# Padding between SBUF tiles, whole-chunk transposes and a new pitch for the hidden features in an attention and mixture-of-experts kernel

## The chip, the cores and the metric

The kernel runs on one core of one Trainium2 chip. The metric is the device time of one execution in microseconds (us). Before the change it is 820.12 us, the median of three runs (819.98 to 822.11).

In a profile PE is TensorE (PEld its weight loads), DVE is VectorE, ACT is ScalarE, POOL is GpSimd and SP is SyncE, whose queue starts most DMAs. L551 is line 551 of the kernel before. In the changed file the lines from 531 to the transposes are one later: L551 is L552 there, and L970 is L971.

## The reference

Three parts follow each other: a causal attention with a decay, a gated dense layer, and eight experts of which each token uses one.

```python
# attention: B, H, S, D = 4, 8, 576, 64
scores = q @ k.T / sqrt(D) + cum[:, None] - cum[None, :]     # cum = cumsum(log(clip(f)))
attn = softmax(where(causal, -1e9, scores)); attn_out = attn @ v
# dense: x has 2304 tokens of 512 features; w1, w2: 512 x 1024; w3: 1024 x 1024; w_out: 1024 x 512
x = ((x @ w1) * (x @ w2)) @ w3 @ w_out
# experts: w1[e]: 512 x 1024, w2[e]: 1024 x 512
e = argmax(x @ w_gate); gate = softmax(x @ w_gate)[e] * sigmoid(x @ w_output_gate)[e]
out = gate * (relu(x @ w1[e]) @ w2[e])
```

Nearly every product is computed in three matmuls on operands that were split into a high and a low part: high times high, high times low, low times high. The split is made by a copy into TensorE's rounded float format (the high part, names with h) and a subtraction of that copy from the value (the remainder or low part, names with l).

## The kernel before

**Attention** takes 16 pairs of heads in a software pipeline whose order is written out by a table of start times. While it runs, pieces of w3 and w_out are read and split as well. The matmuls at L515 to L517 (`product`) then multiply w3 by w_out, so that the dense layer needs one matrix less; their results have the name wc.

**The dense layer** (`gated`, `project`) takes tokens in tiles of 512, 512, 512, 512 and 256. For each tile and each of 8 pieces of the hidden width, 12 matmuls make x @ w1 (name a) and 12 make x @ w2 (name b): 4 pieces of the contraction times the three products of `three` (L551 to L553). ScalarE and VectorE multiply the two and split the product into gh and gl. Then `project` makes the rows y: for each chunk of 128 tokens, 8 pieces times three matmuls with gh or gl as weights and the combined matrix (raw) streaming through. In the first tile the split of w1 and w2 is still going on: VectorE makes the low parts at L467, one pair per piece of the hidden width. The first tile's own split of x is at L571 (ScalarE, high part) and L572 (GpSimd, low part).

**Routing** finds each token's expert and scatters its row to a list per expert in DRAM (L710). The expert with most tokens is done first, in pieces A (256 tokens) and B (128). Seven slots follow, with 344, 320, 320, 296, 280, 256 and 256 tokens each, then a small piece p, then a loop that is empty with this input.

**One slot**: `fetch` reads its token rows from DRAM, in chunks of 128 rows; `features` turns them on TensorE (transposes with the identity, L970), in two runs of two feature blocks each; `layer1` (name h) has 96 matmuls of as many columns as the slot has tokens; `layer2_turned` (name q, 96 matmuls of that width) or `layer2` (name o, 24 matmuls of 512 columns for each chunk of 128 tokens) makes the output rows, which GpSimd scatters. Slots with 320, 320, 296 and 280 tokens use q; A, B and the slots with 344, 256 and 256 use o. Weights of the next slot are read and split meanwhile (`load`, L544 on GpSimd and L545 on VectorE).

**Order.** In this part TensorE and VectorE run in the order in which the code records them (`manual_schedule`). TensorE takes its matmuls strictly in that order; each of them has a weight load of its own, and the load of the next one is done beside the running matmul.

**Where the tiles lie.** Tiles of a pool lie behind each other in SBUF, from the low end or, with side="right", from the high end. The built programs place the start of each tile as follows. Only the remainder modulo 512 bytes is given, and one column of a float32 tile is 4 bytes:

```
tiles                                                        before   after
raw0, raw1 (combined matrix; b weights of odd slots)            128     384
big: w1, w2, gh, gl of the dense layer; other expert weights     32     384
xh, xl of the dense layer's tokens (high end of SBUF)           384     384
cw: the first pieces of w_out and w3                            384     384
gh, gl of an expert slot (pitch 344 columns = 1376 bytes)  416, 288  128, 0
hh, hl of an expert slot (before always pitch 344)         160, 416 384, 128
attention: CK, MR, OQ, tri, junk, PT, vr, ac, ones ...   all 256 higher
attention: kh, kl, qh, ql, kr, qr                             not moved
```

Within raw, big, xh, xl and cw the operands are 512 or 2048 bytes apart, so each of them has the remainder of its tile. The rows of 344 columns are not a whole number of 512 bytes, so each block there has another remainder.

Of the kernel before, what the change touches and what calls it, by code (L numbers as in the profile page):

```python
# [28 lines left out]
P = 128  # L29
# [490 lines left out]
def moe(nc, tc, ident, xT, rz, xs, xpool, raws, region, wc, w1, w2, gates, e1, e2, out):  # L520
# [3 lines left out]
    with (  # L524
# [3 lines left out]
    ):  # L528
        psum = ExitStack()
        st = {"work": wc.work, "unit": 1}  # L530

        def unit(name, n, dt=F32R):

# [428 lines left out]
        def features(nm, g, w):  # L962

            xh = pmb.tile([P, 4, WIN[1]], F32R, name=f"gh{nm}", tag="gxh")
            xl = pmb.tile([P, 4, WIN[1]], F32R, name=f"gl{nm}", tag="gxl")
            yield xh, xl
            for k in range(4):
                pt = mmt(f"gt{nm}{k}") if nm in "A1B" else psx.tile([P, 512], F32, name=f"gt{nm}{k}", tag="x")
                for c, n in chunks(w):
                    PE.transpose(pt[:, P * c:P * c + n], g[0][:n, c, P * k:P * k + P], ident[:n, :n])  # L970
                A.activation(out=xh[:, k, :w], in_=pt[:, :w], func=ACTF.Copy)  # L971
                V.tensor_tensor(out=xl[:, k, :w], in0=pt[:, :w], in1=xh[:, k, :w].bitcast(F32), op=ALU.subtract)
                yield

        def hidden(nm):
            return (pmb.tile([P, 8, WIN[1]], F32R, name=f"hh{nm}", tag="hh"),
                    pmb.tile([P, 8, WIN[1]], F32R, name=f"hl{nm}", tag="hl"))

        def layer1(nm, ws, x, w, h):
            (wh, wl), (xh, xl), (hh, hl) = ws[0], x, h  # L980
# [124 lines left out]
        with tc.manual_schedule(engines={PE_E, DVE_E}):  # L1105
            wm, gA = weights("m", m), fetch("A", rows_of_expert(m), 256)
            fA = features("A", gA, 256)
            xA, hA = next(fA), hidden("A")
            rest = project(len(TT) - 1, TT[-1] // P)
            load(4)  # L1110
            take(fA, 2)
# [25 lines left out]
            run(l1)  # L1137
            y = layer2("A", wm, gA, hA, 256)
            fB = features("B", gB, P)
            xB, hB = next(fB), hidden("B")  # L1140
            run(y)
            run(fB)
            load(2)
# [6 lines left out]
            load(2)  # L1150
            run(layer2("B", wm, gB, hB, P))
            load(1)
            h = hidden("1")
            l1 = layer1("1", ws, x, WIN[1], h)
            for _ in range(3):
                take(l1, 1)
# [2 lines left out]
            for i in range(1, E):  # L1159
                nm, w = str(i), WIN[i]  # L1160
                if i == E - 1:
                    pe0 = nc.values_load(tab[0:1, E:E + 1], engines=SPE, min_val=0, max_val=E - 1)
                    px0 = nc.values_load(tab[0:1, E + MAXP:E + MAXP + 1], engines=SPE, min_val=0, max_val=E * N - R)
                    nm2, e2_, w2_, rows2 = "p", pe0, R, lambda r, n: xs[bass.ds(px0, n)]
                else:
                    nm2, e2_, w2_, rows2 = str(i + 1), slots[i + 1], WIN[i + 1], rows_of_expert(slots[i + 1])
                g2 = fetch(nm2, rows2, w2_)
                ws2 = (weights if i < E - 1 else plain)(nm2, e2_)
                if i > 1:
                    h = hidden(nm)  # L1170
                    l1 = layer1(nm, ws, x, w, h)
                    take(l1)
                for k in range(4):
                    take(l1, 2 if i > 1 else 1)
                    load(1 if i < E - 1 else 0)
                run(l1)
                fx = features(nm2, g2, w2_) if i < E - 1 else iter(())
                x = next(fx, None)
                take(fx, 2)
                y = (layer2_turned if w % P and w <= TURNED else layer2)(nm, ws, g, h, w)  # L1180
                if i < E - 1:
                    take(y)
                    take(fx, 2)
                    for k in range(4):
                        load(1)
                        take(y)
                        take(pl)
                else:
                    x = turned_piece("p", g2)
                    take(y)  # L1190
                    p = piece("p", ws2, g2, x)
                    for _ in range(2):
                        take(p)
                        take(y)
                run(y)
                ws, g = ws2, g2
# [32 lines left out]
def program(shapes):  # L1229
# [3 lines left out]
    with tile.TileContext(nc) as tc:  # L1233
        with tc.tile_pool(name="keep", bufs=1) as keep, tc.tile_pool(name="raws", bufs=2, reuse_waits="tile") as raws, tc.tile_pool(name="div", bufs=1, space=DRAM) as div:
            rz = div.tile([NP, 2, N], F32, name="rz")

            xs = div.tile([E * N, DM + 2], F32, name="xs")
            ident = keep.tile([P, P], F32, name="ident")
            make_identity(nc, ident)
            xpool = ExitStack()  # L1240
            xt = xpool.enter_context(tc.tile_pool(name="xt", bufs=1, side="right"))
            xT = xt.tile([P, NP, N], F32, name="xT")
            region = ExitStack()
            region.enter_context(tc.manual_schedule())
            wc = Combined(nc, tc, xpool, raws, a["wo"], a["w3t"])
            attention(nc, tc, ident, xT, rz, xs, wc, a["q"], a["k"], a["v"], a["f"])
            moe(nc, tc, ident, xT, rz, xs, xpool, raws, region, wc, a["w1"], a["w2"], a["gates"], a["e1"], a["e2"], out)
            xpool.close()
# [10 lines left out]
```

## Time and profile before

| | before |
|---|---|
| median of three runs | 820.12 us (819.98 to 822.11) |
| profiled execution | 821.04 us, its span 819.43 us |
| PE busy | 790.8 us (97%), 5173 matmuls |
| DVE busy | 458.2 us (56%) |
| POOL busy | 349.2 us (43%) |
| ACT busy | 281.6 us (34%) |
| DMA | 102.12 MB, mean 125 GB/s |

The span is what the profiler saw of the device's work, and 1.61 us of the time lie around it. Busy shares are means over stages that differ a lot, so the stage tables below are of more use than this one. A matmul's own duration in the profile overlaps the next one's, so what a matmul costs is the distance from its start to the next start, or the length of a stretch over the matmuls in it.

### The profile page before, as it was taken

Reading aid. Unit: us, or ns where it says so; the run is one execution under the profiler, and the core shown is the slowest. Engines: PE = TensorE matmul, PEld = TensorE weight load, DVE = VectorE, ACT = ScalarE, POOL = GpSimd, SP = SyncE. Lnnn points to the kernel's source line nnn. Section 1 sums busy time; section 2 is a strip of 40 time slices with the busy share of each in tenths; the row PEclk is TensorE's granted clock in tenths of the full one; section 3 lists DMA queues with packets and bytes.
Section 4 is the critical chain, followed back from the end, with each engine's and each line's share of the span. In section 5 each row is a group of like instructions: output and inputs, shape, how many; then the busy total and the mean of one; then the engine's idle time right before and its main releaser. Section 6 shows DMA issues by size and latency. Waiting matters only on the chain.

```text
span 819.4 us, 13839 instructions
## 1 busy us (share of the span) xinstructions
PE 790.8 (97%) x5173; PEld 645.2 (79%) x5173; DVE 458.2 (56%) x971; ACT 281.6 (34%) x536; POOL 349.2 (43%) x362
## 2 busy tenths in 40 slices
PE   8999999998999999999999999999899999999995
PEld 4666667676888887887788788898697999999983
DVE  6788888985999723241341322346367746445520
ACT  2566666553556312212211221313121222322221
POOL 6678889996640210230221011033454443445511
PEclk9999999999999999999999999999999999999998
DMA  3556767524545110110100010044676546547470
GB/s 104 157 156 188 225 213 248 148 67 146 189 155 180 52 40 27 39 38 1 65 7 13 20 39 0 2 151 144 185 242 208 167 176 198 162 166 230 140 267 29
DMA packets 40339, 102.12 MB, mean 125 GB/s; under 512 B 8610, under 2 KB 9314, under 8 KB 40016
## 3 DMA queue, kind: packets, MB, share of 16 engines
q1 hardware_dynamic: 37088, 91.46, 35.2%
q0 software_dynamic: 3184, 9.77, 3.1%
q8 instruction: 41, 0.67, 0.3%
q14 instruction: 26, 0.21, 0.1%
HBM read 84.47 MB, written 16.51 MB: 123 GB/s over the span
## 4 chain that ended last, share of the span: by engine, by line
PE 71%; DVE 10%; DMA 6%; issue 6%; POOL 5%; ACT 1%; SPq 1%; POOLq 0%; DVEq 0%; ACTq 0%
DVE junk L243 6%; PE a L551 4%; PE b L551 4%; PE b L552 4%; PE a L552 4%; PE y L552 4%; PE y L551 4%; PE y L553 4%; PE b L553 4%; PE a L553 4%; PE h L553 3%; PE h L551 3%; PE h L552 3%; PE q L551 2%; DMA out<-ot,id 2%
## 5 line engine op out<-in xcount | busy, mean ns | idle before, releaser
L581 DVE TENSOR_TENSOR ga<-b,ga 128x512 f32<-128x512 f32 (+1 forms) x40 | 25.5, 637 | 149.6 <-PE b L553 148.7
L710 POOL DMA_INDIRECT xs<-xr,pos x18 | 19.0, 1056 | 182.0 <-DVE pos L706 130.6
L243 DVE CUSTOM_DVE_ANT_0 junk<-x,tri 128x256 f32<-128x256 f32 (+3 forms) x128 | 62.7, 490 | 10.6 <-PE x L217 1.5
L551 PE MATMUL h<-gh,ah 128*128 128x320 f32 (+4 forms) x224 | 67.2, 300 | 0.0
L552 PE MATMUL h<-gl,ah 128*128 128x320 f32 (+4 forms) x224 | 66.9, 299 | 0.0
L553 PE MATMUL h<-gh,al 128*128 128x320 f32 (+4 forms) x224 | 66.9, 299 | 0.0
L551 PE MATMUL b<-xh,w2h 128*128 128x512 f32 (+1 forms) x160 | 60.5, 378 | 0.0
L551 PE MATMUL a<-xh,w1h 128*128 128x512 f32 (+1 forms) x160 | 60.3, 377 | 0.0
L552 PE MATMUL b<-xl,w2h 128*128 128x512 f32 (+1 forms) x160 | 60.0, 375 | 0.0
L552 PE MATMUL a<-xl,w1h 128*128 128x512 f32 (+1 forms) x160 | 60.0, 375 | 0.0
L553 PE MATMUL b<-xh,w2l 128*128 128x512 f32 (+1 forms) x160 | 59.3, 371 | 0.0
L553 PE MATMUL a<-xh,w1l 128*128 128x512 f32 (+1 forms) x160 | 59.3, 370 | 0.0
L544 POOL TENSOR_SCALAR bh<-rb 128x1024 fp32r<-128x1024 f32 x28 | 37.0, 1323 | 49.0 <-DMA rb<-e 43.9
L285 POOL TENSOR_SCALAR_AFFINE_SELECT PT<-PT 128x256 f32<-128x256 f32 (+1 forms) x80 | 45.6, 584 | 28.9 <-ACT PT L279 27.0
L551 PE MATMUL y<-raw,gh 128*128 128x512 f32 x144 | 57.6, 400 | 0.0
L552 PE MATMUL y<-raw,gh 128*128 128x512 f32 x144 | 57.0, 396 | 0.0
L553 PE MATMUL y<-raw,gl 128*128 128x512 f32 x144 | 56.7, 393 | 0.0
L583 ACT ACTIVATE gh<-ga 128x512 fp32r<-128x512 f32 (+1 forms) x40 | 23.6, 589 | 90.8 <-DVE ga L581 90.8
L986 DVE SCALAR_TENSOR_TENSOR hl<-h,hh 128x320 fp32r<-128x320 f32 (+4 forms) x56 | 25.4, 463 | 48.0 <-ACT hh L985 46.3
L306 PE MATMUL v<-PT,vr 128*64 128x448 f32 (+4 forms) x384 | 49.8, 396 | 1.1 <-ACT zs L329 1.1
L545 DVE TENSOR_TENSOR bl<-rb,bh 128x1024 fp32r<-128x1024 f32 x28 | 37.9, 1376 | 15.0 <-POOL bh L544 15.0
L297 POOL TENSOR_TENSOR ac<-ac,PT 128x640 f32<-128x640 f32 (+1 forms) x32 | 45.6, 1424 | 1.6
(611 smaller groups left out, 2177.6 us busy)
## 6 DMA issues: line engine op xcount, KB each, us to landing
ra<-e SPq DMA_DIRECT2D x28, 512.0 KB
rb<-e SPq DMA_DIRECT2D x28, 512.0 KB
w<-w3t SPq DMA_DIRECT2D x16, 512.0 KB
xs<-zero SPq DMA_DIRECT2D x8, 771.0 KB
vr<-v SPq DMA_DIRECT2D x16, 320.0 KB
kr<-k SPq DMA_DIRECT2D x16, 288.0 KB
qr<-q SPq DMA_DIRECT2D x16, 288.0 KB
wo<-wo SPq DMA_DIRECT2D x8, 512.0 KB
```

The lines of the kernel that those rows point to most:

```text
L243: V.tensor_tensor_reduce(out=junk[:, :w], in0=s["x", i][:, 512 * h:512 * h + w] if i < 4 else s["x", i][:, 224:224 + S], in1=tri[:, 640 - ...
L285: G.affine_select(out=t, in_=t, pattern=[[0, 2], [1, w]], compare_op=ALU.is_ge, fill=0.0, base=0, channel_multiplier=-1,)
L297: G.tensor_tensor(out=acc[:, :, q0 - P:], in0=first if j == 1 else acc[:, :, q0 - P:], in1=src, op=ALU.add)
L306: PE.matmul(s["v"][HALF[h], 384 + q0:384 + q1], s["vr"][:, j, HALF[h]], place(s, j, h, q0, q1), start=(j == 0), stop=(j == 4 or q1 == P),)
L544: G.tensor_scalar(out=hi, in0=src, scalar1=1.0, scalar2=1.0, op0=ALU.mult, op1=ALU.mult)
L545: lo_eng.tensor_tensor(out=lo, in0=src, in1=hi.bitcast(F32), op=ALU.subtract)
L551: PE.matmul(ps, ah, bh, start=start and i == 0, stop=False)
L552: PE.matmul(ps, ah, bl, start=False, stop=False)
L553: PE.matmul(ps, al, bh, start=False, stop=stop and i == last)
L581: V.tensor_tensor(out=ga[:, :w], in0=pb[:, :w], in1=ga[:, :w], op=ALU.mult)
L583: A.activation(out=gh[:, f, :w], in_=ga[:, :w], func=ACTF.Copy)
L986: V.scalar_tensor_tensor(out=hl[:, f, :w], in0=ps[:, :w], scalar=0.0, in1=hh[:, f, :w].bitcast(F32), op0=ALU.max, op1=ALU.subtract)
```

## The change

It is described as three changes: tiles at one address modulo 512 bytes, whole-chunk transposes of gathered rows, and the first tile's remainders on VectorE.

- Three tiles that nothing uses are added as padding (24 columns in pool mo2, 72 in mob, 64 in keep), and with them the tiles lie as in the table above.
- The hidden features of a slot of at most 256 tokens have a pitch of 256 columns instead of 344; the calls of `hidden` hand over the number of tokens.
- The transposes of the last chunk of a slot's rows take all 128 rows instead of the slot's last 88, 64, 40 or 24. The rows were read by `fetch` before as well; the copies behind the transposes read the same columns as before.
- For the third part there is no edit in the diff. The split at L571 and L572 is the same in both files.

```diff
@@ moe
         st = {"work": wc.work, "unit": 1}
+        p2.tile([P, 24], F32, name="shift2", bufs=1)
@@ features
-                for c, n in chunks(w):
-                    PE.transpose(pt[:, P * c:P * c + n], g[0][:n, c, P * k:P * k + P], ident[:n, :n])
+                for c, _ in chunks(w):
+                    PE.transpose(pt[:, P * c:P * c + P], g[0][:, c, P * k:P * k + P], ident)
@@ hidden
-        def hidden(nm):
-            return (pmb.tile([P, 8, WIN[1]], F32R, name=f"hh{nm}", tag="hh"),
-                    pmb.tile([P, 8, WIN[1]], F32R, name=f"hl{nm}", tag="hl"))
+        def hidden(nm, w):
+
+            pitch = WIN[-1] if w <= WIN[-1] else WIN[1]
+            made = [pmb.tile([P, 8 * WIN[1]], F32R, name=f"{x}{nm}", tag=x) for x in ("hh", "hl")]
+            if "shift" not in st:
+                st["shift"] = pmb.tile([P, 72], F32, name="shift3")
+            return tuple(t[:, :8 * pitch].rearrange("p (f c) -> p f c", c=pitch) for t in made)
...
@@ program
             ident = keep.tile([P, P], F32, name="ident")
+            keep.tile([P, 64], F32, name="shift")
```

The order of instructions moves in one place of its kind on one engine. On PE, between the last matmuls of layer 1 of the slot with 344 tokens (h) and the first of its layer 2 (o), the transposes (gt) of the next slot's gathered rows (xg, 320 tokens) stood like this before:

```order
L553 MATMUL h_6274<-gh_5997,al_5864 128x344
L970 MATMUL gt_6291<-ident,xg_6182 128x128 x2
L970 MATMUL gt_6291<-ident,xg_6182 128x64
L970 MATMUL gt_6297<-ident,xg_6182 128x128 x2
L970 MATMUL gt_6297<-ident,xg_6182 128x64
L551 MATMUL o_6303<-bh_5865,hh_6079 128x512
```

and stand like this now:

```order
L554 MATMUL h_6277<-gh_6000,al_5867 128x344
L971 MATMUL gt_6294<-ident,xg_6185 128x128 x3
L971 MATMUL gt_6300<-ident,xg_6185 128x128 x3
L552 MATMUL o_6306<-bh_5868,hh_6082 128x512
L553 MATMUL o_6306<-bl_5869,hh_6082 128x512
```

The number of transposes is the same; the third of each three is 128 columns wide instead of 64. There are ten such runs, two for each of the slots with 344, 320, 320, 296 and 280 tokens.

On POOL, in the part where the last pieces of w3 and w_out are split (L467) and the first tile's x is split, the low parts of that tile (xl) stood like this before:

```order
L467 TENSOR_TENSOR raw_76<-wo7u,raw_76 128x512
L572 TENSOR_TENSOR xl_2994<-xT,xh_2993 128x512 x2
L467 TENSOR_TENSOR raw_77<-w07u,raw_77 128x512
L572 TENSOR_TENSOR xl_2994<-xT,xh_2993 128x512
L467 TENSOR_TENSOR raw_77<-w17u,raw_77 128x512
```

and stand like this now:

```order
L467 TENSOR_TENSOR raw_77<-wo7u,raw_77 128x512
L573 TENSOR_TENSOR xl_2996<-xT,xh_2995 128x512 x2
L467 TENSOR_TENSOR raw_78<-w07u,raw_78 128x512
L573 TENSOR_TENSOR xl_2996<-xT,xh_2995 128x512
L467 TENSOR_TENSOR raw_78<-w17u,raw_78 128x512
```

Nothing moved there: the remainders stay on GpSimd. DVE, ACT, POOL and SP have the same instructions in the same order in both programs, apart from line and buffer numbers.

## Rows read from the trace of the kernel before

**Rows 1.** Stages of the span: us, then busy (count) by engine, PEclk, DMA share, GB/s.
```profile
0.00:193.34 193.34, 177.17 (x1813) 123.84 (x1814) 161.05 (x397) 109.05 (x173) 159.02 (x172) 0.99 0.54 168
193.34:237.14 43.80, 43.80 (x196) 36.16 (x193) 37.27 (x42) 22.25 (x39) 27.76 (x18) 1.00 0.48 156
237.14:519.14 282.00, 282.00 (x1268) 224.89 (x1266) 111.54 (x253) 74.74 (x145) 44.28 (x48) 1.00 0.13 44
519.14:601.58 82.44, 78.62 (x514) 68.09 (x512) 41.83 (x123) 22.04 (x59) 26.51 (x39) 1.00 0.42 132
601.58:810.82 209.24, 209.24 (x1393) 192.26 (x1391) 106.46 (x158) 53.03 (x121) 90.65 (x85) 1.00 0.57 189
```

**Rows 2.** Groups of 512-column matmuls by line and shape: busy us, mean ns.
```profile
L551 PE MATMUL y<-raw,gh 128*128 128x512 f32 x144 | 57.6, 400 | 0.0
...
L551 PE MATMUL b<-xh,w2h 128*128 128x512 f32 x128 | 51.2, 400 | 0.0
L551 PE MATMUL a<-xh,w1h 128*128 128x512 f32 x128 | 51.0, 399 | 0.0
```

**Rows 3.** Stretches of 512-column matmuls: wc, wc, wc, a and b, y.
```profile
204.35:215.24 10.89, 10.89 (x49) 9.01 (x48) 10.23 (x12) 4.89 (x9) 6.71 (x4) 1.00 0.56 182
218.00:228.88 10.88, 10.88 (x49) 9.01 (x48) 10.85 (x11) 6.05 (x11) 8.95 (x6) 1.00 0.50 165
228.88:231.69 2.81, 2.81 (x13) 2.26 (x12) 2.81 (x2) 1.19 (x2) 2.35 (x2) 1.00 0.25 102
237.14:281.94 44.80, 44.80 (x193) 36.04 (x192) 40.71 (x71) 24.97 (x43) 1.32 (x2) 1.00 0.44 141
281.94:293.14 11.20, 11.20 (x49) 8.96 (x48) 8.80 (x25) 1.23 (x2) 8.16 (x10) 1.00 0.04 4
```

**Rows 4.** Stretches of narrower matmuls: a and b of 256, q of two 320 slots.
```profile
533.91:545.43 11.52, 11.52 (x98) 11.52 (x97) 3.40 (x8) 3.21 (x8) 1.95 (x2) 1.00 0.54 182
651.01:654.64 3.63, 3.63 (x26) 3.62 (x25) 2.01 (x4) 0.44 (x1) 2.38 (x2) 1.00 0.66 176
...
682.84:686.46 3.62, 3.62 (x26) 3.61 (x26) 1.99 (x4) 0.42 (x1) 2.25 (x2) 1.00 0.66 171
```

**Rows 5.** Timeline of PE at four runs of transposes: start, us, line, operation, count.
```profile
593.57 0.76 PE L970 MATMUL gt<-ident,xg 128*128 128x128 f32 x6
594.17 0.49 PE L1006 MATMUL htB<-ident,hrB 128*128 128x128 f32 x3
...
616.73 1.15 PE L970 MATMUL gt<-ident,xg 128*128 128x128 f32 x6
617.80 0.50 PE L551 MATMUL o<-bh,hh 128*128 128x512 f32 x1
...
716.92 1.08 PE L970 MATMUL gt<-ident,xg 128*128 128x128 f32 x6
717.94 0.41 PE L551 MATMUL q<-hh,bh 128*128 128x296 f32 x1
...
767.57 0.60 PE L970 MATMUL gt<-ident,xg 128*128 128x128 f32 x4
767.92 0.48 PE L551 MATMUL o<-bh,hh 128*128 128x512 f32 x1
```

**Rows 6.** Timeline of DVE, then PE: last weights of the first dense tile.
```profile
273.52 1.74 DVE L467 TENSOR_TENSOR w1l<-wa7u,w1h 128x512 fp32r<-128x512 f32 x1
...
276.81 0.39 PE L553 MATMUL a<-xh,w1l 128*128 128x512 f32 x1
```

**Rows 7.** Timeline of PE where it waits between pieces A and B.
```profile
577.56 0.51 PE L551 MATMUL oA<-bhm,hhA 128*128 128x512 f32 x1 [1.05 <-POOL bhm L544]
...
587.13 0.66 PE L970 MATMUL gtB<-ident,xgB 128*128 128x128 f32 x4 [1.28 <-DMA xgB<-xs]
```

**Rows 8.** The group of the page that the attention waits for most.
```profile
L243 DVE CUSTOM_DVE_ANT_0 junk<-x,tri 128x256 f32<-128x256 f32 (+3 forms) x128 | 62.7, 490 | 10.6 <-PE x L217 1.5
```

More of the change, by code (lines that the diff above doesn't have):

```diff
@@ L1107, in moe @@
             fA = features("A", gA, 256)
-            xA, hA = next(fA), hidden("A")
+            xA, hA = next(fA), hidden("A", 256)
             rest = project(len(TT) - 1, TT[-1] // P)
@@ L1139, in moe @@
             fB = features("B", gB, P)
-            xB, hB = next(fB), hidden("B")
+            xB, hB = next(fB), hidden("B", P)
             run(y)
@@ L1152, in moe @@
             load(1)
-            h = hidden("1")
+            h = hidden("1", WIN[1])
             l1 = layer1("1", ws, x, WIN[1], h)
@@ L1169, in moe @@
                 if i > 1:
-                    h = hidden(nm)
+                    h = hidden(nm, w)
                     l1 = layer1(nm, ws, x, w, h)
```

## The prediction

> **What bounds the kernel now.** I read the busy time by stage first [rows 1]. [...] From 519.14 to 601.58 PE is idle for 82.44 - 78.62 = 3.8 us, at waits inside the pieces A and B. Before 193.34 us the attention is a chain through all engines; PE is busy for 177 of 193 us there and DVE for 161, and no single engine's speed sets it. Behind PE's last matmul stand 8.6 us of copy, scatter and closing. [...]
>
> **What a matmul costs, and what address has to do with it.** Next I compared stretches with the same work in each matmul (512 columns, a 128 x 128 weight load beside it) and different addresses [rows 3]. A stretch counts one matmul that began before it, so its number is the count less one.
> - 204.35 to 215.24 us: 48 matmuls in 10.89 us, 226.9 ns each. The streaming operand lies at 384 modulo 512, the weights at 128: 256 apart.
> - 218.00 to 228.88 us: 48 in 10.88 us, 226.7 ns. Both at 32.
> - 228.88 to 231.69 us: 12 in 2.81 us, 234.2 ns. Same line, same loop, weights at 128 and streaming at 32.
> - 237.14 to 281.94 us (a and b of the first tile): 192 in 44.80 us, 233.3 ns. Weights at 32, streaming at 384.
> - 281.94 to 293.14 us (y): 48 in 11.20 us, 233.3 ns. Weights at 32, streaming at 128.
> [...] The third line decides for me that it is the address: it stands in the middle of the same product and differs in nothing else that I see. After the change all of raw, big, xh, xl and cw lie at 384, so a, b and y should run at 226.7.
>
> [...]
>
> **The change part by part**, each on PE's path.
> 1. a and b of the four tiles of 512: 6 groups of 128 matmuls, 768 [rows 2], by 233.3 - 226.7 = 6.6 ns: -5.1 us.
> 2. y: 3 groups of 144, 432 [rows 2], by 6.6 ns: -2.9 us.
> 3. a and b of the last tile: 192 of 256 columns, 120.0 ns each (96 in 11.52 us) [rows 4]. No row shows this width at equal addresses. Bounds: nothing, and the same 6.6 ns (-1.3 us). I take half, as the columns are half: -0.6 us.
> 4. o: with pitch 256 the weights hh and hl lie at 384 or 128 and the streaming weights of the slot at 384, so equal modulo 256. The two slots of 256 tokens and B have 48 + 48 + 24 = 120 such matmuls: -0.8 us. A has 48 more, but PE waits in them for bhm, and behind them for the gather xgB [rows 7]; both hang on scatters, not on PE's speed. So A gains nothing. The slot with 344 tokens keeps its pitch, where each block has another remainder: 0.
> 5. q (384 matmuls): the hidden features keep pitch 344, so their blocks go through all remainders, whatever the weights' is. The rows have the test: the slot at 651.01 us has weights at 32 and needs 3.63 us for its first quarter, that at 682.84 us has them at 128 and needs 3.62 [rows 4]. I take 0.
> 6. h (768 with A): streaming gh and gl have pitch 344, and their remainders against the weights' only change places. Taken 0; no row has another arrangement, so the bounds are 6.6 ns scaled to some 300 of 512 columns, 3.9 ns each, 3.0 us to either side.
> 7. The wc stretch at 228.88 us: -0.1 us.
> 8. Transposes. A run of six with 64 or fewer columns in the last chunk takes 1.07 us from its start to the next matmul's (616.73 to 617.80), in the slot of 280 tokens 1.02 (716.92 to 717.94) [rows 5]; the eight such runs take 1.07, 1.10, 1.08, 1.08, 1.05, 1.04, 1.02 and 1.02, together 8.46 us. The run with 88 columns in the last chunk takes 0.60 (593.57 to 594.17), and four whole ones 0.35 (767.57 to 767.92). So the narrow ones do not save columns; they cost some 0.2 us each. Six whole ones are bounded by 1.5 x 0.35 = 0.53 and by 0.60 with two wider transposes, 0.66. I take 0.59: 8 x 0.59 = 4.7, so -3.7 us (bounds -4.2 and -3.2). The two runs of the 344 slot change by less than 0.1 us.
> [...]
>
> Sum: -(5.1 + 2.9 + 0.6 + 0.8 + 0.1 + 3.7) = -13.2 us.
>
> **What could be late next.** VectorE makes the weights of the first dense tile while PE uses them. The last low part of w1 ends at 273.52 + 1.74 = 275.26 us and is first needed at 276.81 [rows 6]. PE reaches that place 7 x 24 x 6.6 ns = 1.1 us earlier, with 0.1 from part 7: 1.55 - 1.2 leaves 0.3 us. That just holds. If VectorE's part comes 1 us late, 1 us is lost once. The gathers, scatters and weight loads around A and B start when PE or engines behind it are done, so they move along; only what PE gains between two of their steps is lost, which part 4 has left out.
> Third part of the description: nothing in the program does it, so it is 0 for certain.
> Attention: the two operands of each matmul there move together, or one moves by 256, so no pair changes modulo 256; DVE's, ACT's and POOL's work is the same. 0.
>
> The sum is made on the profiled execution: 821.04 - 13.2 = 807.8 us. That execution is 0.92 us above the median of the runs, to which the result will be compared: 820.12 - 13.2 = 806.9 us, which I forecast.
>
> **The rivals.**
> - *Address does not matter.* wc goes to another PSUM bank after each three matmuls, a and b put 12 and y 24 into one, and that might make the difference. Then only the transposes count: 820.1 - 3.7 = 816.4 us. Against it stands the stretch at 228.88 us, which changes banks too and is slow. Chance 0.08.
> - *The gain is partly swallowed by waits.* VectorE limits the first tile (1.3 us of part 1), and the last tile's gain ahead of A (part 3, and 48 of the y: 0.9 us) goes into longer waits there: 806.9 + 2.2 = 809.1 us. For it: the margin of 0.3 us. Against it: the weights and the scatters follow PE. Chance 0.15.
> - *h gains as well*, since remainders that change places need not cost the same: 806.9 - 3.0 = 803.9 us. Nothing in the rows speaks for it. Chance 0.06.
> - *Slower than before.* In the attention 256 bytes move the tiles of VectorE's scan for maxima (junk, tri) against the tiles at the high end of SBUF. If engines meet in SBUF by address as TensorE's two reads do, these instructions, 128 of 490 ns (62.7 us, on the chain) [rows 8], would stretch. They must cost 13.2 us more, that is 21%, before the kernel is slower; at 25% it would be 822.6 us. For it: the chain waits for VectorE there. Against it: their operands move by the same 256 bytes, and nothing else about them changes. Chance 0.03.
>
> **How the numbers follow.** The forecast has 0.68, the rivals 0.32. The likeliest one's own range is 804 to 810 us (parts 3, 6 and 8 with their bounds). With the swallowed gain, 803.5 to 811.5 us; outside are the first and the last rival and some of the tails, 0.2. About 0.3% (2.5 us) is what this measurement can tell from no change. The forecast and three rivals are faster than that, the first rival by only 3.7 us, so that a part of it may read as no change: faster 0.93, same 0.04, slower 0.03.
>
> **What would show it.** In the changed kernel's profile a and b of the first tile should take 43.5 us instead of 44.80 for 192 matmuls, and y 10.88 instead of 11.20 for 48; a run of six transposes 0.6 us everywhere; an o of the last slots 226.7 ns a matmul. PE should have no idle time between 193 and 519 us, and waits of about the same length at A and B. q and h should stay within 1% per matmul. It is wrong if a and b stay at 233 ns (first rival), if PE shows idle time in the first tile (second), if h changes by more than 2 ns a matmul, or if the attention does not end at 193 us within 1 us.

## The result and the profile after

The changed kernel takes 809.49 us (median of four runs, 808.69 to 811.58), beside 820.05 us of the kernel before (four runs, 818.91 to 822.11). The ratio is 0.9872, with a 95% interval of 0.9845 to 0.9899. A second comparison (the last experiment below) gave 808.79 against 820.10 us, 0.9854 with 0.9824 to 0.9884. So 10.6 and 11.3 us went, where 13.2 were forecast; 809.49 lies inside the stated range (803.5 to 811.5), 2.6 us above the forecast of 806.9.

The stages of the changed kernel's profiled execution (808.69 us, span 807.0), cut at the same instructions as [rows 1] and with the same columns:

```profile
0.00:192.15 192.15, 176.75 (x1812) 123.26 (x1814) 160.46 (x397) 108.84 (x173) 158.05 (x172) 1.00 0.54 169
192.15:235.80 43.65, 43.65 (x196) 36.14 (x193) 35.34 (x40) 20.31 (x36) 26.55 (x18) 1.00 0.47 147
235.80:512.07 276.27, 275.82 (x1267) 224.66 (x1266) 112.33 (x255) 76.28 (x147) 45.04 (x48) 1.00 0.13 46
512.07:593.70 81.63, 77.89 (x513) 68.11 (x512) 41.96 (x123) 22.06 (x59) 26.39 (x39) 1.00 0.42 132
593.70:798.42 204.72, 204.72 (x1393) 191.81 (x1391) 105.97 (x159) 52.05 (x121) 87.31 (x85) 1.00 0.59 193
```

Stage by stage the difference is -1.2 us (attention), -0.15 (product), -5.7 (dense tiles of 512), -0.8 (last tile, A and B) and -4.5 (the seven slots): 12.4 in all. Before the change PE was busy for the whole of the second, the third and the last stage, at a granted clock of 1.00 [rows 1]; there the time is the sum of the distances between matmul starts, so the price was taken on PE from the product on. PE is still busy for the whole of the second and the last stage; in the third it is now idle for 276.27 - 275.82 = 0.45 us, which it was not.

The rows y of the first tile (48 matmuls), and 96 matmuls of a and b of the last tile, in the changed kernel; they answer to [rows 3] and [rows 4]:

```profile
280.26:291.14 10.88, 10.88 (x49) 8.96 (x48) 8.52 (x21) 1.23 (x2) 8.13 (x10) 1.00 0.04 4
525.46:536.98 11.52, 11.52 (x98) 11.52 (x97) 3.79 (x12) 3.22 (x8) 1.95 (x2) 1.00 0.56 183
```

512 columns went from 233.3 to 226.7 ns a matmul, as forecast. 256 columns stayed at 11.52 us for 96, a mean of 120.0 ns. The transposes, timeline of PE of the changed kernel (they answer to [rows 5]):

```profile
608.90 0.82 PE L971 MATMUL gt<-ident,xg 128*128 128x128 f32 x6
609.48 0.48 PE L552 MATMUL o<-bh,hh 128*128 128x512 f32 x1
...
701.81 0.82 PE L971 MATMUL gt<-ident,xg 128*128 128x128 f32 x6
702.38 0.38 PE L552 MATMUL q<-hh,bh 128*128 128x296 f32 x1
```

A run of six takes 0.58 us from its start to the next matmul's in the slot of 320 and 0.57 in that of 280, where it took 1.07 and 1.02.

The new idle time stands at the first b of the first tile. PE's timeline, then VectorE's, of the changed kernel:

```profile
238.30 0.39 PE L554 MATMUL a<-xh,w1l 128*128 128x512 f32 x1
239.13 0.50 PE L552 MATMUL b<-xh,w2h 128*128 128x512 f32 x1 [0.45 <-DVE raw L771]
```
```profile
234.47 2.47 DVE L771 TENSOR_TENSOR raw<-wc,raw 128x512 fp32r<-128x512 f32 x4
...
238.40 2.47 DVE L771 TENSOR_TENSOR raw<-wc,raw 128x512 fp32r<-128x512 f32 x4
```

L771 takes the results wc out of PSUM, and the first b waits until the first of the second four has been read. With the matmuls behind it that start late, the first tile loses 0.94 us there: its a and b take 44.46 us instead of the 43.52 that 192 x 226.7 ns make.

PE's waits inside A and B in the changed kernel (they answer to [rows 7]), and the attention's group of [rows 8]:

```profile
570.37 0.50 PE L552 MATMUL oA<-bhm,hhA 128*128 128x512 f32 x1 [1.39 <-POOL bhm L545]
...
579.34 0.66 PE L971 MATMUL gtB<-ident,xgB 128*128 128x128 f32 x4 [0.84 <-DMA xgB<-xs]
```
```profile
L243 DVE CUSTOM_DVE_ANT_0 junk<-x,tri 128x256 f32<-128x256 f32 (+3 forms) x128 | 62.6, 489 | 9.9 <-PE x L217 0.7
```

The scan in the attention takes 489 ns where it took 490: the rival of a slower attention is out.

### The profile page after: what moved, and what is told of

It reads as the page before. It is cut to its first block, busy times and chain, and to the rows that moved or that the text cites. A ratio compares the mean times of both kernels' runs of the same rounds, so it can differ in the third digit from the quotient of the medians.

```text
span 807.0 us, 13835 instructions
## 1 busy us (share of the span) xinstructions
PE 778.8 (97%) x5171; PEld 644.0 (80%) x5173; DVE 456.1 (57%) x971; ACT 280.0 (35%) x536; POOL 344.3 (43%) x362
## 4 chain that ended last, share of the span: by engine, by line
PE 63%; DVE 14%; DMA 10%; issue 6%; POOL 4%; ACT 2%; SPq 0%; POOLq 0%; DVEq 0%; ACTq 0%
DVE junk L243 6%; PE b L552 4%; PE y L552 4%; PE y L554 4%; PE b L554 4%; PE a L552 4%; PE b L553 4%; PE y L553 4%; PE a L554 4%; PE a L553 4%; DMA out<-ot,id 3%; PE h L552 3%; PE h L554 3%; PE h L553 3%; POOL ac L297 2%
## 5 line engine op out<-in xcount | busy, mean ns | idle before, releaser
L552 PE MATMUL y<-raw,gh 128*128 128x512 f32 x144 | 56.8, 395 | 0.0
L553 PE MATMUL y<-raw,gh 128*128 128x512 f32 x144 | 56.0, 389 | 0.0
```

The costliest lines, as they stand in the source:

```text
L552: PE.matmul(ps, ah, bh, start=start and i == 0, stop=False)
L553: PE.matmul(ps, ah, bl, start=False, stop=False)
```

## The experiments

A kernel with one time was run once, with a profile; where there is an interval it was timed in five rounds beside the kernel before. A length per matmul is again a stretch over its matmuls.

**The padding alone.** The changed kernel without the whole-chunk transposes and without the pitch of 256:

```diff
-                for c, _ in chunks(w):
-                    PE.transpose(pt[:, P * c:P * c + P], g[0][:, c, P * k:P * k + P], ident)
+                for c, n in chunks(w):
+                    PE.transpose(pt[:, P * c:P * c + n], g[0][:n, c, P * k:P * k + P], ident[:n, :n])
...
-            pitch = WIN[-1] if w <= WIN[-1] else WIN[1]
+            pitch = WIN[1]
```

> The changed kernel with its three padding tiles, but with the old transposes of part chunks and the old pitch of 344 columns for all hidden features. Theory (the address modulo 256 sets the rate of 512-column matmuls): a and b of the first tile at 226.7 ns each (192 in 43.5 us plus any wait), y at 226.7 (48 in 10.88 us), o of the last two slots still at 233 to 237 ns, the eight narrow runs of transposes still 8.4 us together. The time is that of the changed kernel plus 3.9 us (transposes) plus 0.7 us (o): 814 us, ratio to before 0.993. Rival (address does not matter, the changed kernel's gain comes from elsewhere): a and b at 233.3 ns, 820 us, ratio 1.000.

Measured: 813.95 us against 821.07, ratio 0.9914 (0.9894 to 0.9933). Its a and b, and y, of the first tile, and PE's wait for B's rows:

```profile
236.89:280.41 43.52, 43.52 (x194) 36.04 (x193) 40.35 (x71) 25.22 (x43) 1.32 (x2) 1.00 0.43 145
280.41:291.30 10.89, 10.89 (x50) 8.97 (x49) 8.53 (x21) 1.23 (x2) 8.14 (x10) 1.00 0.03 4
```
```profile
580.94 0.78 PE L971 MATMUL gtB<-ident,xgB 128*128 128x128 f32 x4 [2.38 <-DMA xgB<-xs]
```

Three unused tiles are worth 7.1 us, and the rate of 226.7 ns is all theirs. What the pitch of 256 is worth can be read here too: with 344 the 48 o of each of the last two slots take 11.28 and 11.64 us, in the changed kernel 11.10 and 11.43.

The wait for the gather xgB is 2.38 us here, 0.84 in the changed kernel, 1.28 before [rows 7], and in the next kernel's profile PE does not wait there at all. In this profile the granted clock is 0.50 from just behind that wait:

```profile
581.33:584.75 3.42, 3.42 (x10) 2.53 (x9) 2.12 (x6) 0.79 (x4) 3.20 (x4) 0.50 0.20 75
```

The 24 matmuls hB that follow take 7.07 us instead of the 5.68 of the changed kernel's profile. In the next kernel's profile the clock is at 0.50 ahead of the place, from 578.9 to 582.3 us, so PE comes later and finds the rows there. From A's first o to the transposes of B's rows it is 14.98 us before, 14.63 in the changed kernel, 16.07 here and 15.34 in the next kernel: a difference of a microsecond around A and B in one profile says nothing on an edit.

**The transposes alone.** The kernel before, with one edit:

```diff
-                for c, n in chunks(w):
-                    PE.transpose(pt[:, P * c:P * c + n], g[0][:n, c, P * k:P * k + P], ident[:n, :n])
+                for c, _ in chunks(w):
+                    PE.transpose(pt[:, P * c:P * c + P], g[0][:, c, P * k:P * k + P], ident)
```

> The kernel before with whole-chunk transposes as the only edit. Theory: each of the eight narrow runs takes 0.58 us instead of 1.02 to 1.10, together -3.8 us; a, b and y stay at 233.3 ns: 816.2 us, ratio 0.9953. Rival (the narrow transposes were cheap and the runs got short because of the addresses): runs stay near 1.05 us, 820 us, ratio 1.000.

Measured: 816.57 us against 821.07, 0.9944 (0.9926 to 0.9961), -4.5 us. In its slots the eight runs are shorter by 3.9 us, as in the changed kernel; a and b stay at 233.3 ns. PE's timeline at one run:

```profile
616.87 0.82 PE L970 MATMUL gt<-ident,xg 128*128 128x128 f32 x6
617.44 0.48 PE L551 MATMUL o<-bh,hh 128*128 128x512 f32 x1
```

The two parts make 11.6 us, 7.1 and 4.5. The changed kernel, which has the pitch as well, gained 10.6 and 11.3; within the intervals, 1.4 to 2.5 us to either side, that agrees with parts that add up. In this profile the first b waits as well (0.87 us for L770), though the addresses are those of before: PE left the attention 2.0 us earlier than in the profile of before, and VectorE's second four at L770 start at 238.44 us, where it was 238.58 before.

**The third part, as described.** The changed kernel, and the first tile's remainders on VectorE:

```diff
-                    G.tensor_tensor(out=xl[:, k, :w], in0=xv, in1=xh[:, k, :w].bitcast(F32), op=ALU.subtract)
+                    V.tensor_tensor(out=xl[:, k, :w], in0=xv, in1=xh[:, k, :w].bitcast(F32), op=ALU.subtract)
```

> The changed kernel with the third part of its description added: the four low parts of the first tile's x are made by VectorE instead of GpSimd. Theory (in the first dense tile PE is held by VectorE, which is busy from 232 to 247 us without a break and made PE wait 0.45 us at the first b): four more instructions of about 0.7 us on VectorE ahead of that place make the wait longer, up to 2.8 us: 810.5 to 812.5 us, ratio to before 0.988 to 0.991. Rival (GpSimd is what is late there): the wait of 0.45 us and the 0.17 us behind it go, 808.9 us, ratio 0.9864.

Measured: 808.62 us against 821.07, 0.9849 (0.9828 to 0.9869). The loss that I expected did not come, and whether there is a small gain can't be told from 0.9872 (0.9845 to 0.9899) and 0.9854 of the changed kernel. Why VectorE may have room for four more instructions is seen in the changed kernel, on VectorE and on GpSimd:

```profile
227.60 1.77 DVE L460 SCALAR_TENSOR_TENSOR wb0u<-wb,wb0u 128x512 int32<-128x512 int32 x1
...
237.47 0.68 DVE L460 SCALAR_TENSOR_TENSOR wb1u<-wb,wb1u 128x512 int32<-128x512 int32 x1
```
```profile
227.09 1.74 POOL L573 TENSOR_TENSOR xl<-xT,xh 128x512 fp32r<-128x512 f32 x1
228.78 1.75 POOL L467 TENSOR_TENSOR raw<-w17u,raw 128x512 fp32r<-128x512 f32 x1
...
235.02 1.30 POOL L467 TENSOR_TENSOR w2l<-wb0u,w2h 128x512 fp32r<-128x512 f32 x1 [0.76 <-ACT w2h L465]
```

The same instruction takes 1.77 us while GpSimd subtracts, and 0.68 at 237.47 us, when GpSimd's last subtraction has ended (236.32) and it is idle. So a subtraction taken over from GpSimd would cost VectorE its own time and give some of it back. That this is why nothing was lost is argued, not shown.

**Equal addresses for the other widths.** The features and the hidden features of the slots get pitches that are whole multiples of 256 bytes:

```diff
-            xh = pmb.tile([P, 4, WIN[1]], F32R, name=f"gh{nm}", tag="gxh")
+            pitch = next(p for p in (256, 320, WIN[1]) if w <= p)
+            xh = pmb.tile([P, 4 * WIN[1] + 32], F32R, name=f"gh{nm}", tag="gxh")
...
-            pitch = WIN[-1] if w <= WIN[-1] else WIN[1]
+            pitch = next(p for p in (256, 320, WIN[1]) if w <= p)
```

> The changed kernel with the features and the hidden features of slots with up to 320 tokens at a pitch of 320 or 256 columns, and the features' tiles 128 bytes longer, so that in h and q the two operands of each matmul have the same address modulo 256 as well. Theory 1 (equal addresses help at each width, in proportion to the columns): 672 h and 384 q matmuls by some 3.9 ns, -4.1 us: 805.4 us, ratio 0.9822; q of 320 columns at 143 ns instead of 147. Theory 2 (the penalty is there with 512 columns only; a and b of the last tile, 256 columns, took 120.0 ns before and after): h and q within 1 ns of what they are, 809.5 us, ratio 0.9872.

Measured: 810.42 us against 821.07, 0.9870 (0.9849 to 0.9891): no better than the changed kernel. From the first h of the slots to PE's last matmul it takes 205.4 us, the changed kernel 204.7. The first quarters of q with 320 tokens stay within 0.01 us. Against the changed kernel the 96 h of a slot are 0.1 us shorter with 320 tokens, 0.4 longer with 280 (its q 0.3 longer) and 0.2 longer with 256. In these runs equal addresses help matmuls of 512 columns (226.7 against 233.3 ns), and the widths from 256 to 320 by 0.1 us in 96 matmuls or not at all. That fits term 3 of the prediction, which came out as nothing.

**How far apart.** Five paddings that put the two operands of a, b and y at other distances; everything else is the changed kernel. The first three:

```diff
-        p2.tile([P, 24], F32, name="shift2", bufs=1)
+        p2.tile([P, 40], F32, name="shift2", bufs=1)
```
```diff
-            keep.tile([P, 64], F32, name="shift")
+            keep.tile([P, 32], F32, name="shift")
```
```diff
-            keep.tile([P, 64], F32, name="shift")
```

> One padding tile is 40 columns instead of 24: w1, w2, gh and gl of the dense layer lie at 448 modulo 512, x and the combined matrix stay at 384. The two operands of a, b and y are 64 bytes apart. Theory (a 512-column matmul is dear as soon as its operands differ modulo 256): a and b 12 in 2.80 us instead of 2.72, y 48 in 11.20 instead of 10.88. Rival (only distances like the 96 bytes of before are dear, the memory is divided into larger pieces): 64 apart stays at 2.72 and 10.88. The a and b of the last tile (256 columns) stay at 120.0 ns by both.

> One padding tile is 32 columns instead of 64: w1, w2, gh, gl and the combined matrix lie at 256 modulo 512, x stays at 384. The operands of a and b are 128 bytes apart, those of y have the same address modulo 512. Theory (equality modulo 256 decides): a and b 12 in 2.80 us, y 48 in 10.88. Rival (equality modulo 128 is enough): a and b in 2.72 as well, so nothing is lost against the changed kernel.

> The third padding tile is left out: w1, w2, gh, gl and the combined matrix lie at 128 modulo 512, x stays at 384. The operands of a and b are 256 bytes apart, those of y equal. Theory (modulo 256): a and b 12 in 2.72 us, y 48 in 10.88, as in the changed kernel. Rival (it is modulo 512, as the change is described): a and b in 2.80, y in 10.88.

Measured, 64 apart (818.84 us, 1.6 of them a low clock at the start of the product, which the last experiment deals with, and 1.6 more a low clock in piece B): a and b of the first tile, y, and 108 matmuls of the last tile:

```profile
238.72:283.52 44.80, 44.80 (x194) 36.10 (x192) 40.41 (x70) 24.92 (x43) 1.85 (x2) 1.00 0.43 141
283.52:294.72 11.20, 11.20 (x49) 8.97 (x48) 8.79 (x25) 1.23 (x2) 8.15 (x10) 1.00 0.04 4
533.80:546.04 12.24, 12.24 (x111) 12.24 (x109) 4.01 (x13) 3.60 (x9) 1.95 (x2) 1.00 0.55 187
```

128 apart with y equal (814.37 us, with the same 1.6 at the start of the product), the same three:

```profile
237.52:282.32 44.80, 44.80 (x194) 36.04 (x193) 40.47 (x70) 24.97 (x43) 1.85 (x2) 1.00 0.42 141
282.32:293.22 10.90, 10.90 (x50) 8.97 (x49) 8.55 (x22) 1.23 (x2) 8.13 (x10) 1.00 0.03 4
530.42:543.28 12.86, 12.86 (x111) 12.86 (x110) 3.98 (x13) 3.59 (x9) 1.95 (x2) 1.00 0.53 174
```

256 apart with y equal (808.24 us), a and b, and y:

```profile
236.19:279.71 43.52, 43.52 (x194) 36.04 (x192) 40.52 (x71) 25.23 (x43) 1.33 (x2) 1.00 0.43 145
279.71:290.59 10.88, 10.88 (x49) 8.96 (x48) 8.52 (x21) 1.23 (x2) 8.13 (x10) 1.00 0.04 4
```

At 512 columns it went as the theory said: 256 apart is as good as equal, 64 and 128 are as bad as before. So it is the address modulo 256, and "modulo 512" in the description asks for more than is needed. One figure fell out of both: the last tile, 64 apart, runs at 12.24 / 108 = 113.3 ns, faster than at equal addresses (120.0). So equality is not the best at every width. The other two paddings look for better distances, below zero:

```diff
-            keep.tile([P, 64], F32, name="shift")
+            keep.tile([P, 40], F32, name="shift")
...
-        p2.tile([P, 24], F32, name="shift2", bufs=1)
+        p2.tile([P, 32], F32, name="shift2", bufs=1)
```

(72 and 8 columns in the second.)

> Two padding tiles are changed (40 instead of 64 columns, 32 instead of 24): w1, w2, gh, gl lie at 320 modulo 512, the combined matrix at 288, x at 384. The weights of a and b start 64 bytes below the streaming operand (192 modulo 256), those of y 32 above. Theory one (equality modulo 256 is the one good place at 512 columns, every other distance gives 233.3 ns): a and b 12 in 2.80 us, y 48 in 11.20. Theory two (the distance only sets when the two reads meet, as the last tile's 113.3 ns at 64 bytes apart instead of 120.0 at equal addresses suggests, so there may be better places than equality): one of them under 226.7 ns, 220 being the next step of 6.7: a and b 2.64, or y 10.56. The last tile's a and b (256 columns) tell how that width likes 192: 113.3 or 120.0.

> The two padding tiles have 72 and 8 columns: w1, w2, gh, gl lie at 352 modulo 512, the combined matrix at 416, x at 384. The weights of a and b start 32 bytes below the streaming operand (224 modulo 256), those of y 64 below (192). Theory one (only equality is good): a and b 12 in 2.80 us, y 48 in 11.20. Theory two (some other distance is better still): a and b 2.64, or y 10.56; y must then agree with what a and b show at 192 in the other kernel of this pair, since the distance decides and not the tiles. The last tile's a and b: 113.3 or 120.0 ns.

Measured, the first (812.79 us): a and b, y, last tile; then the second (813.21 us): 12 of b, y, last tile:

```profile
237.04:280.99 43.95, 43.95 (x193) 36.06 (x192) 40.30 (x70) 25.07 (x43) 1.86 (x2) 1.00 0.44 144
280.99:292.18 11.19, 11.19 (x50) 8.97 (x49) 8.78 (x25) 1.23 (x2) 8.14 (x10) 1.00 0.04 4
528.98:541.69 12.71, 12.71 (x110) 12.71 (x109) 3.97 (x13) 3.59 (x9) 1.95 (x2) 1.00 0.54 187
```
```profile
244.94:247.74 2.80, 2.80 (x14) 2.25 (x13) 2.80 (x6) 2.65 (x5) 0.00 (x0) 1.00 0.27 42
281.34:292.34 11.00, 11.00 (x50) 8.96 (x48) 8.63 (x22) 1.23 (x2) 8.15 (x10) 1.00 0.03 4
...
530.09:542.81 12.72, 12.72 (x110) 12.72 (x109) 3.98 (x13) 3.60 (x9) 1.95 (x2) 1.00 0.52 186
```

Neither theory holds as written. No distance beats equality at 512 columns, but 192 is a middle one: 43.95 / 192 = 228.9 ns for a and b, and 11.00 / 48 = 229.2 for y in the other kernel, so the distance decides and not the tiles. All distances, worked out from these rows, [rows 3] and [rows 4] (ns a matmul; start of the weights less start of the streaming operand, modulo 256 bytes):

```
distance       0      32      64      96     128     160     192     224
512 columns  226.7  233.1   233.3   234.2   233.3   233.3   229.0   233.3
256 columns  120.0    -     113.3     -     119.1   120.0   117.7   117.8
```

The entry for 96 rests on 12 matmuls, that for 32 on the 48 of one stretch. Most entries are means of unequal steps from start to start: 233.3 before the change is made of steps of 231 to 232 and of 237 to 238 ns, and 120.0 at distance 160 of steps between 115 and 125. Even steps are seen at distance 0 (226 to 227 ns with 512 columns, 120 with 256), and 113 to 114 ns for most matmuls at 64 with 256.

**Where the transposes' cost lies.** The narrow transposes are back, but the two blocks of a run are interleaved, so that the two narrow ones stand together:

```diff
+            for k in (0, 2):
+                pt = [psx.tile([P, 512], F32, name=f"gt{nm}{k + i}", tag="x") for i in range(2)]
+                for c, n in chunks(w):
+                    for i in range(2):
+                        PE.transpose(pt[i][:, P * c:P * c + n], g[0][:n, c, P * (k + i):P * (k + i) + P], ident[:n, :n])
```

> The transposes of the slots' last chunks take the slot's last 88, 64, 40 or 24 rows again, as before the change, but the two blocks of a run are interleaved, so that the two narrow transposes of a run stand next to each other, behind four whole ones; everything else is as changed. Theory (what is dear is the change between 128 rows and 64 or fewer, paid on entering and leaving): a run of six takes some 0.83 us, half of the excess of 1.07 over 0.58. Rival (each narrow transpose is dear by itself): 1.07 us, as before. If both fall, the runs are at 0.58 and it was something else in the order.

Measured: 810.37 us, and on PE's timeline:

```profile
608.83 0.86 PE L981 MATMUL gt<-ident,xg 128*128 128x128 f32 x6
609.62 0.50 PE L552 MATMUL o<-bh,hh 128*128 128x512 f32 x1
```

The run takes 0.79 us, in the slots of 296 and 280 tokens 0.77 and 0.76: half of the excess is gone with half of the changes between 128 rows and 64, 40 or 24, though as many narrow transposes run. So it is the change that costs, about 0.1 us each way. The single steps in the trace say the same. Two whole transposes start 108 to 110 ns apart. Before the change a narrow one starts 201 to 204 ns behind a whole one, and what follows it starts 167 to 206 ns later; in this kernel the second narrow one starts 83 to 112 ns behind the first. It is the rows that are read and not the columns that are made: the transposes of the results at L1071 of the kernel before alternate 128 with 64, 40 or 24 columns of the array at 128 rows, and start 108 to 110 ns apart throughout.

What TensorE does in the 0.1 us no run here shows.

**A version from these findings, and the changed kernel again.** The remainders on VectorE, and distance 64 for matmuls of 256 columns: the last tile's x starts 48 columns further in, and the features of A and of the slots with 256 tokens have a pitch of 320 columns and their own starts.

```diff
+            o = 48 if t == len(TT) - 1 else 0
...
+            pitch, offs = {256: (320, (48, 16)), P: (320, (0, 32))}.get(w, (WIN[1], (0, 0)))
```

> The changed kernel with three additions: the first tile's remainders of x are made on VectorE; the x of the last tile lies 192 bytes further in its tile, so that its 256-column matmuls (a and b) have weights 64 bytes above the streaming operand; and the features of A and of the two slots with 256 tokens have a pitch of 320 columns and such a start that the same distance of 64 holds for each block of h. Theory (the best distance depends on the width: 0 at 512 columns, 64 at 256): a and b of the last tile 113.3 ns instead of 120.0 (192 matmuls, -1.3 us), h of A and of the last two slots some 113.5 instead of 118.8 (288, -1.5 us), so 806.7 us, and 805.8 with the 0.9 us by which the remainders on VectorE seemed better. Rival one (what comes ahead of A's waits is swallowed there): only the last two slots gain, -1.0, and -0.9: 807.6. Rival two (h has another order of weights than a and b, and 64 is nothing special for it): h stays at 118.8.

> The changed kernel once more, on the same chip and beside the same runs of before as the kernel of this pair. Theory (the wait of the first b for VectorE and the low clock at the start of the product come and go with the end of the attention): the same 809.5 us within 1, and in this profile other values for these two: a first b that waits 0 to 1.1 us, and 48 matmuls of the product's first half in 11.0 or in 12.6 us. Rival (the wait of the first b belongs to the change): again about 0.7 us lost there.

Measured, on one chip: the version 808.38 us, 0.9848 (0.9817 to 0.9879); the changed kernel 808.79, 0.9854 (0.9824 to 0.9884); before 820.10. The version's last tile, its slot 6 (96 h) and its slot 7 (96 h); then the two slots in the first profile of the changed kernel:

```profile
524.35:536.59 12.24, 12.24 (x111) 12.24 (x110) 4.01 (x13) 3.61 (x9) 1.95 (x2) 1.00 0.52 172
742.97:753.96 10.99, 10.99 (x99) 10.99 (x97) 4.50 (x9) 4.29 (x10) 5.29 (x6) 1.00 0.40 136
765.79:777.19 11.40, 11.40 (x98) 11.27 (x96) 4.38 (x9) 3.39 (x8) 2.74 (x5) 1.00 1.00 376
```
```profile
744.39:755.80 11.41, 11.41 (x99) 11.41 (x97) 4.93 (x10) 4.28 (x10) 5.26 (x5) 1.00 0.42 141
767.61:778.99 11.38, 11.38 (x97) 11.24 (x96) 4.34 (x9) 3.39 (x8) 2.59 (x5) 1.00 0.98 360
```

The last tile runs at 113.3 ns, as expected, and slot 6 gained 0.42 us; A's h, among other matmuls, gained 0.25, half of what was hoped for. Slot 7, with the same distance, gained nothing. What differs there in the rows is that DMA is busy for all of slot 7 (1.00 against 0.40). Against DMA as the cause stands that its steps are an even 117 to 119 ns from the first to the last, and that slot 6 has 113 to 114 ns already in its first quarter, where the DMA share is 0.73. It was not tried, and the cause stays open. In time the version can't be told from the changed kernel (0.4 us apart, intervals that overlap): a gain that the profile shows can't be seen among the differences between executions.

Those differences are seen in the second profile of the changed kernel. Its first tile, the first 11 us of the product with the stretch from 193.2 us on, and PE's timeline at the first b; last the first 11 us of the product in the first profile:

```profile
237.44:280.96 43.52, 43.52 (x194) 36.05 (x192) 40.23 (x70) 25.15 (x43) 1.85 (x2) 1.00 0.43 145
...
192.18:203.20 11.02, 11.02 (x45) 8.95 (x42) 5.24 (x9) 4.73 (x9) 5.08 (x4) 0.85 0.38 108
...
193.20:196.00 2.80, 2.80 (x8) 2.16 (x7) 0.00 (x0) 1.93 (x5) 2.15 (x2) 0.50 0.10 30
```
```profile
240.16 0.39 PE L552 MATMUL b<-xh,w2h 128*128 128x512 f32 x1
```
```profile
192.15:203.17 11.02, 11.02 (x53) 9.12 (x50) 5.18 (x9) 4.39 (x9) 5.10 (x4) 1.00 0.38 108
```

The first b does not wait, and a and b take 43.52 us. But the product begins at a granted clock of 0.50, so that 11 us hold 45 matmuls instead of 53; the first 48 take 12.6 us, 1.6 more, and PE comes to its first b that much later. So this profile alone does not say whether the wait belongs to the change. The others do: in five more kernels with a, b and y at equal addresses modulo 256 (padding alone, equal addresses for the other widths, 256 apart, narrow transposes together, the version from these findings) the product ran at a granted clock of 1.00 and a and b of the first tile took 43.52 us, while the kernel with the transposes alone, at the old addresses, waited. The wait is no part of the change.

It does not come with the end of the attention either, as I had expected. The product began at 192.15 us in the first profile and at 192.29 with the narrow transposes together. What differs is VectorE. ScalarE's copy of the first piece of w1, then VectorE's second four at L771, in the first profile:

```profile
221.10 0.66 ACT L456 ACTIVATE wa0u<-wa 128x512 f32<-128x512 f32 x1 [2.49 <-DMA wa<-w]
```

(the second four are shown above, at 238.40) and with the narrow transposes together:

```profile
219.15 0.68 ACT L456 ACTIVATE wa0u<-wa 128x512 f32<-128x512 f32 x1 [1.38 <-DMA wa<-w]
...
237.40 2.47 DVE L771 TENSOR_TENSOR raw<-wc,raw 128x512 fp32r<-128x512 f32 x4
...
238.68 0.39 PE L552 MATMUL b<-xh,w2h 128*128 128x512 f32 x1
```

In the first profile the piece is copied 2.0 us later, behind a longer wait for its DMA, and VectorE's second four start 1.0 us later: that is the first b's loss. VectorE's second four start at 238.40 or 238.44 us in the three profiles with a late first b, and at 237.3 to 237.6 in four that left the attention at 192.3 to 192.5 us and had no wait. Why the DMA lands later was not tried.

The low clock at the start of the product happened in 4 of the 14 profiles. PE had been idle for 1.9 us just ahead of the attention's last matmuls in both profiles of the changed kernel, so that wait alone does not tell them apart. In 4 other profiles the clock was at 0.50 for as long around A and B, as in the padding alone above.

## Why the prediction was right, and where it was not

That 512-column matmuls get shorter at equal addresses modulo 256 held for the change that was made (226.7 against 233.3 ns), and the two large terms were nearly right. What makes the distance between the operands count, a meeting of two reads as the prediction has it or something else, no run shows; the runs show the step at each distance. The rule behind the two terms, one price at equal addresses modulo 256 and another at any other distance, was too simple: at 512 columns 192 has a price in between (229.0 ns), and at 256 columns 64 is better than equality. By the steps:

- **Terms 1 and 2** (a, b and y, -8.0 us): 6.6 ns a matmul is what uninterrupted stretches gain (44.80 to 43.52 us for 192, 11.20 to 10.88 for 48). Next to other matmuls less is gained: the first 12 of b in a later tile went from 2.98 to 2.95 us, y's groups of 24 from 5.68 to 5.58, 4.2 ns each. From the first y to the last tile it was 5.4 us, with 1.28 of the first tile and 0.27 of the last y 6.9 in all. The term was too large by 1.1 us, since all 1200 matmuls got the rate of the best 240.
- **Term 3** (last tile, -0.6): failed in its size; it is 0. I scaled the gain by the columns, but at 256 columns equal addresses and 160 apart cost the same mean of 120.0 ns.
- **Term 4** (o, -0.8): -0.64. The 24 of B went from 5.97 to 5.83 us; the slots of 256 gave 0.26 and 0.24.
- **Terms 5 and 6** (q and h): q moved by 0.02 us a quarter at most. h went up by 0.05 to 0.07 us in four slots and down by 0.04 to 0.12 in three, together nothing. The bounds of 3 us were not needed.
- **Term 7** (-0.1): -0.15.
- **Term 8** (transposes, -3.7): -3.9, with 0.05 lost in the slot of 344.
- **What could be late next**: the margin was looked for at the wrong place. The last weights held; the first b did not, in one profile of the changed kernel of two (0.94 us). Of the profiles in which PE left the attention at 192.1 to 192.3 us and the granted clock stayed at 1.00, it waited where VectorE's second four at L771 came at 238.4 us, and did not where they came at 237.3 to 237.4. The second rival's mechanism was real in that profile, its place another.
- **A and B**: the waits moved by some tenths either way (oA 1.05 to 1.39, gtB 1.28 to 0.84), as said. That A gains nothing is not what this profile shows: from its first o to B's transposes it is 14.98 us before and 14.63 after, with waits that are 0.1 us shorter in sum. As that stretch differs by more than a microsecond between profiles, whether A keeps the gain is open.
- **Attention**: it ended 1.2 us earlier, outside the 1 us that the prediction had set for itself. This is no effect of the change: with the attention's tiles where they were before it ended at 193.34, 191.30 and 192.53 us (before, transposes alone, 256 apart), with the tiles of the table 256 bytes higher at 192.15 to 193.38.

The median came nearer to the second rival's 809.1 us than to the forecast, but not by that rival's sum: 0.9 of its 2.2 us was to be lost ahead of A. Of what is short of 13.2 us, 1.1 are in terms 1 and 2 and 0.6 in term 3; the wait at the first b had 0.94 in one profile of two, and the rest is not settled. The likeliest case's range, 804 to 810 us, is narrower than its three bounds added up (802.7 to 811.0); the result lies in both.

From the product's start on the profile is shorter by 11.2 us, and by 12.1 without the wait at the first b. That the medians differ by 10.6 and 11.3 only is open to a microsecond. How often that wait came in the timed runs is not known. The low clock does not favour one kernel there: the mean granted clock of the timed runs is 0.993 to 0.998 for the changed kernel and 0.989 to 0.998 for the one before, with medians of 0.995 and 0.995.

## What to carry to other kernels

Where PE is busy throughout, measure the distance between matmul starts in stretches that differ in one thing: 6.7 ns on 512 columns were read off the kernel before and worth 7 us for three unused tiles. Price such a rate only on stretches like those it was read from: matmuls among others gained less (2.5 and 4.2 ns in two such places), and matmuls of 256 columns nothing (120.0 ns before and after). And do not let whole transposes alternate with ones of 64, 40 or 24 rows, or put the narrow ones together: each change cost about 0.1 us, while 88 rows cost nothing extra (0.60 us for the run with them, 0.58 for six whole ones). Before a wait in one profile is put down to an edit, look at it in several profiles: the first b waited in 3 of 14, with the new addresses and with the old.

## What the runs showed of the hardware that was not expected

- The best distance between the two operands depends on the matmul's width: 0 modulo 256 at 512 columns (226.7 ns against 233.3), 64 at 256 columns (113.3 against 120.0 at distance 0).
- A start address alone does not fix the price: at distance 64 the h of one slot took 114.5 ns a matmul and of the next 118.8.
- A transpose of 64, 40 or 24 rows between transposes of 128 costs about 0.1 us on entering and on leaving; one of 88 rows does not (it starts 108 ns behind a whole one, and the next starts 53 to 80 ns later), and fewer columns of the array at 128 rows do not either (108 to 110 ns from start to start).
- The granted clock fell to 0.50 for some 3.4 us at the start of the product in 4 of 14 profiles, after an attention of the same length, and cost 1.6 us each time; in 4 others it fell around A and B.
